# A recurrence and a long convolution on one core: states decimated by two, spilled to DRAM, and the two branches interleaved

## The chip, the cores and the metric

The kernel runs on one core of a Trainium2 chip. The metric is the device time of one execution in microseconds (us), as the median of several runs. The engines are called TensorE (PE in the profile; PEld is its weight load), VectorE (DVE), ScalarE (ACT), GpSimd (POOL) and SyncE (SP). In this kernel SyncE computes nothing: it issues nearly all DMAs, in program order.

## The reference, cut to what matters

The output mixes two branches over a sequence of 2048 steps and 1024 channels in bf16. Branch A (called S5 below) is a complex diagonal recurrence. Branch B multiplies a 4-tap shift convolution of k with v and runs the product through a 2048-long convolution, by a transform of length 4096. A gate per time step mixes them.

```python
g = sigmoid((x * gate_w).sum(-1, keepdims=True))
# branch A (S5)
Lam_bar = exp(dt * Lam);  B_bar = ((Lam_bar - 1) / Lam)[:, None] * Bmat
Bu = einsum("bld,pd->blp", x, B_bar)
for t in range(L):                       # 2048 steps, 1024 complex states
    h = Lam_bar * h + Bu[:, t, :]
a = 2 * einsum("blp,dp->bld", hseq, Cmat).real + x * Dskip
# branch B (convolution)
kv = shift_conv4(k, shift_k) * v
y  = irfft(rfft(pad(kv)) * rfft(pad(ssm_k)))[:, :S] + kv * ssm_D
b  = x * y
out = g * a + (1 - g) * b
```

## The kernel before

It computes branch B first and branch A after it, in two separate phases.

The convolution works on eight units of 128 channels. Each unit has a first transform stage (`stage1`), a spectrum stage (`spec`), a product on VectorE, an inverse (`inverse`) whose result is spread over partitions by DMA into `zb`, and a final stage. All PSUM tiles come from one pool of four, and their evictions are split between VectorE ("V") and ScalarE ("A").

```python
with tc.tile_pool(name="bpsum", bufs=4, space=PSUM) as bpsum, ...:
    def inverse(pp, zb, q, eng):
        ps = bpsum.tile([128, 4, 2, CH], F32, name="ps")
        ...                                              # [cut: 12 matmuls]
        qq = bW.tile([128, 4, 2, CH], BF16, name="qq")   # pool bW: 2 buffers
        evac(eng, qq, ps)
        for i in range(4):
            nc.sync.dma_start(out=zb[...], in_=qq[:, i]...)
    ...
    for u in range(NU):                                  # 8 units
        zb = bZ.tile([128, 16, 2, CH], BF16, name="zb")  # pool bZ: 2 buffers
        for q in range(4):
            spec(z, kv, q, 0, "A")
            stage1(a, zs[u + 1], w, 2 * (q % 2), "V")
            ...                                          # [cut]
            inverse(*pend, "A")
            final(zb_prev, u - 1, q - 2, "V" if q == 2 else "A")
```

Then comes the recurrence, in four time blocks of 512 steps. C is transposed whole and scaled; each block runs the input GEMM, rotates *every* step on VectorE, scans it, rotates it back, and runs the output GEMM from states that never leave SBUF:

```python
for pi in range(NP):
    ...                                                  # [cut] CrT, CiT: 16 transposes, 4 x 8 scalings on ScalarE
for tb in range(NTB):                                    # 4 time blocks
    for pi in range(NP):                                 # 8 state blocks
        ...                                              # [cut] 16 input matmuls, 2 evictions
        nc.vector.tensor_tensor(out=t1, in0=tbc, in1=bure, op=ALU.mult)        # rotate: 6 ops of 512
        ...
        nc.vector.tensor_tensor_scan(out=Wre, data0=rcol_bc, data1=pre_re, initial=init_re, ...)
        nc.vector.tensor_tensor_scan(out=Wim, data0=rcol_bc, data1=pre_im, initial=init_im, ...)
        ...                                              # rotate back: 6 ops of 512
    for tl in range(TT_B):
        ...                                              # [cut] output GEMM of a time tile, gate, store
```

## Time and profile before

| | before |
|---|---|
| time, median of 2 runs | 644.14 us (643.22 to 645.06) |
| TensorE busy | 410.0 us, 64% |
| VectorE busy | 465.4 us, 72% |
| ScalarE busy | 306.4 us, 48% |
| moved by DMA | 59.4 MB |

Lines of the page of the kernel before. The first lines give busy time and share of each engine; the next four show, in 40 equal slices of the span (16 us each), the busy tenths of TensorE and VectorE, the granted TensorE clock in tenths, and the busy share of the DMA engines; the last is a group of instructions (busy us, mean ns | idle before them, and what ended it).

```profile
span 643.4 us, 6726 instructions
...
PE 410.0 (64%) x2240; PEld 212.4 (33%) x2240; DVE 465.4 (72%) x1059; ACT 306.4 (48%) x415; POOL 4.1 (1%) x10
...
PE   0023877484747493953451087999699978998577
...
DVE  7649997393939462630372389999999899989952
...
PEclk9999997778887888876875578999889998999579
DMA  9899705564749364135994022041204200110001
...
L283 DVE CAST zkv<-ps 128x1024 bf16<-128x1024 f32 x28 | 34.2, 1220 | 50.0 <-PE ps L327 49.8
```

The window table of the same kernel, by stage: length of the window, then busy us of each engine with its instruction count, the granted clock, the DMA share and the rate.

```profile
core 0: us, PE busy (x) PEld busy (x) DVE busy (x) ACT busy (x) POOL busy (x), PEclk, DMA share, GB/s
0.00:41.00 41.00, 0.00 (x0) 0.00 (x0) 21.47 (x63) 22.20 (x26) 4.10 (x10) 1.00 0.94 146
41.00:298.00 257.00, 156.10 (x1080) 104.66 (x1080) 168.42 (x267) 134.56 (x139) 0.00 (x0) 0.85 0.58 123
298.00:372.00 74.00, 23.20 (x76) 8.28 (x77) 28.92 (x62) 50.05 (x61) 0.00 (x0) 0.64 0.60 120
372.00:622.00 250.00, 213.42 (x1005) 91.82 (x1005) 240.67 (x655) 92.75 (x180) 0.00 (x0) 0.91 0.16 49
```

What TensorE waited for in the convolution stage of the same kernel (total us, times, longest):

```profile
engine line waited for: us in total, times, longest us
PE ps L327 <- DMA va<-kv_scr: 55.7, 6, 13.1
...
PE ps L374 <- DMA zb<-qq: 20.5, 5, 5.8
```

The tables are read together. Between 41 and 298 us the convolution runs alone and no engine is busy for more than two thirds: it is a chain of waits (reload of `va`, arrival of `zb`), and the clock is granted at 0.85 only. Between 372 and 622 us VectorE is busy 240.7 of 250 us: it is the bound there. So each phase leaves idle what the other needs.

A measure used below is *column work*: the moving columns of all matmuls in a window times 0.216 us per 512 columns, the spacing of matmuls at the full clock in this trace. The kernel before has about 346 us of it in 643 us.

### The profile page before, as it was taken

What the parts mean: (1) busy time and instruction counts of PE and PEld (TensorE: products, weight loads), DVE (VectorE), ACT (ScalarE), POOL (GpSimd) and SP (SyncE); (2) the same over time, 40 slices, a digit from 0 to 9 for tenths busy, and PEclk for the clock granted to TensorE, in tenths of its full rate; (3) what the DMA queues carried; (4) which work ended last, traced back from release to release, by engine and by line L of the source; (5) the groups of instructions that cost most, each with busy time, mean ns of one, the idle gap of its engine ahead of it and who ended that gap; (6) DMA issues with size and microseconds to landing.
All of it is one profiled execution on the core that took longest, in us unless ns stands there. A gap on an engine that the chain in (4) does not pass through costs nothing.

```text
span 643.4 us, 6726 instructions
## 1 busy us (share of the span) xinstructions
PE 410.0 (64%) x2240; PEld 212.4 (33%) x2240; DVE 465.4 (72%) x1059; ACT 306.4 (48%) x415; POOL 4.1 (1%) x10
## 2 busy tenths in 40 slices
PE   0023877484747493953451087999699978998577
PEld 0011654252424362631110033344244433443133
DVE  7649997393939462630372389999999899989952
ACT  3832865454454664741369961264126611552042
POOL 2000000000000000000000000000000000000000
PEclk9999997778887888876875578999889998999579
DMA  9899705564749364135994022041204200110001
GB/s 173 154 163 254 164 26 131 120 143 100 162 84 175 70 131 89 43 98 103 169 201 116 17 83 59 7 131 66 63 4 130 83 0 1 52 64 0 2 16 49
DMA packets 166026, 59.44 MB, mean 92 GB/s; under 512 B 142312, under 2 KB 158696, under 8 KB 165992
## 3 DMA queue, kind: packets, MB, share of 16 engines
q1 hardware_dynamic: 157312, 54.54, 39.6%
q10 hardware_dynamic: 8680, 4.48, 2.8%
q8 instruction: 17, 0.28, 0.2%
q14 instruction: 17, 0.14, 0.1%
HBM read 17.06 MB, written 12.58 MB: 46 GB/s over the span
## 4 chain that ended last, share of the span: by engine, by line
DVE 41%; PE 21%; ACT 11%; DMA 9%; SPq 9%; issue 5%; ACTq 0%; DVEq 0%
DVE Wim L575 5%; DVE Wre L573 5%; DMA va<-kv_scr 4%; SPq L363 4%; PE ps L336 3%; ACT kv L285 3%; PE ps L327 3%; DVE acc L306 2%; PE psy L607 2%; PE psy L604 2%; PE ps L356 2%; SPq L491 2%; DVE pre_re L549 2%; DVE pre_im L555 2%; DVE hb_re L584 1%
## 5 line engine op out<-in xcount | busy, mean ns | idle before, releaser
L285 ACT CAST kv<-ps 128x1024 bf16<-128x1024 f32 x64 | 64.3, 1015 | 65.8 <-PE ps L338 58.3
L283 DVE CAST zkv<-ps 128x1024 bf16<-128x1024 f32 x28 | 34.2, 1220 | 50.0 <-PE ps L327 49.8
L327 PE MATMUL ps<-tab_188,va 128*128 128x256 bf16 x128 | 25.4, 341 | 57.5 <-DMA va<-kv_scr 55.7
L336 PE MATMUL ps<-zkv,fC 128*128 128x512 bf16 x128 | 54.7, 428 | 6.2 <-ACT kv L285 4.9
L604 PEld LDWEIGHTS <-hb_re 128*128 128x128 bf16 x256 | 25.7, 102 | 76.2 <-DVE hb_re L584 46.1
L285 ACT CAST qq<-ps 128x1024 bf16<-128x1024 f32 x32 | 32.5, 1019 | 32.1 <-DMA zb<-qq 29.6
L327 PE MATMUL ps<-tab_188,ka 128*128 128x256 bf16 x128 | 20.9, 295 | 42.0 <-DVE ka L321 41.4
L285 ACT CAST zkv<-ps 128x1024 bf16<-128x1024 f32 x36 | 36.1, 1022 | 22.1 <-PE ps L327 22.0
L607 PEld LDWEIGHTS <-hb_im 128*128 128x128 bf16 x256 | 26.1, 103 | 47.6 <-issue 18.4
L542 ACT ACTIVATE bure<-bu_re 128x512 bf16<-128x512 f32 x32 | 19.1, 597 | 47.3 <-PE bu_re L535 18.5
L613 ACT ACTIVATE m_t<-dsk,gcols 128x512 bf16<-128x512 bf16 x32 | 23.1, 723 | 35.6 <-DVE u_t L617 32.7
L611 ACT ACTIVATE ga<-psy,gcols 128x512 bf16<-128x512 f32 x32 | 21.3, 676 | 38.6 <-PE psy L607 37.5
L337 PE MATMUL ps<-zkv,fS 128*128 128x256 bf16 x128 | 38.4, 300 | 0.0
L338 PE MATMUL ps<-zkv,fN 128*128 128x256 bf16 x128 | 38.3, 299 | 0.0
L356 PE MATMUL ps<-pp,gC 128*128 128x256 bf16 x128 | 32.5, 288 | 8.6 <-ACT kv L285 5.0
L327 PEld LDWEIGHTS <-va 128*128 128x128 bf16 x128 | 14.9, 120 | 64.2 <-DMA va<-kv_scr 57.5
L374 PE MATMUL ps<-zb,tabFc 128*128 128x512 bf16 x32 | 15.1, 473 | 28.7 <-DMA zb<-qq 28.7
L573 DVE TENSOR_TENSOR_SCAN Wre<-rv,init_re,pre_re 128x512 bf16<-128x512 f32 x24 | 30.6, 1276 | 0.0
L575 DVE TENSOR_TENSOR_SCAN Wim<-rv,init_im,pre_im 128x512 bf16<-128x512 f32 x24 | 30.5, 1271 | 0.0
L543 ACT ACTIVATE buim<-bu_im 128x512 bf16<-128x512 f32 x32 | 19.1, 596 | 22.5 <-PE bu_im L538 22.5
L306 DVE TENSOR_TENSOR acc<-acc,tmpj 128x2047 bf16<-128x2047 bf16 (+2 forms) x24 | 29.3, 1222 | 0.5
L357 PE MATMUL ps<-pp,gN 128*128 128x128 bf16 x128 | 29.2, 228 | 0.0
(793 smaller groups left out, 1153.3 us busy)
## 6 DMA issues: line engine op xcount, KB each, us to landing
zb<-qq SPq DMA_DIRECT2D x128, 64.0 KB
ka<-in_B_ssm_k_dram SPq DMA_DIRECT2D x8, 512.0 KB
kv_scr<-acc SPq DMA_DIRECT2D x8, 512.0 KB
va<-kv_scr SPq DMA_DIRECT2D x8, 512.0 KB
pB_scr<-cv SPq DMA_DIRECT2D x16, 256.0 KB
out_dram<-ot SPq DMA_DIRECT2D x16, 256.0 KB
pbb<-pB_scr ACTq DMA_DIRECT2D x8, 256.0 KB
x_tt<-in_A_x_dram SPq DMA_DIRECT2D x8, 256.0 KB
```

The source lines that it names most:

```text
L283: nc.vector.tensor_copy(o, i_)
L285: nc.scalar.copy(o, i_)
L306: nc.vector.tensor_tensor(out=acc[:, j:S], in0=acc[:, j:S], in1=tmpj[:, 0:S - j], op=ALU.add)
L327: nc.tensor.matmul(ps[:, i, :], lhsT=a[:, 4 * q + i, :], rhs=t1v, start=True, stop=True)
L336: nc.tensor.matmul(ps[:, i], lhsT=fC[:, k2, :], rhs=z[:, k2], start=True, stop=False)
L337: nc.tensor.matmul(ps[:, i, :, 0, :], lhsT=fS[:, k2, :], rhs=z[:, k2, :, 1, :], start=False, stop=False)
L338: nc.tensor.matmul(ps[:, i, :, 1, :], lhsT=fN[:, k2, :], rhs=z[:, k2, :, 0, :], start=False, stop=True)
L356: nc.tensor.matmul(ps[:, i], lhsT=gC[:, k2, :], rhs=pp[:, i], start=True, stop=False)
L573: nc.vector.tensor_tensor_scan(out=Wre, data0=rcol_bc, data1=pre_re, initial=init_re, op0=ALU.mult, op1=ALU.add)
L575: nc.vector.tensor_tensor_scan(out=Wim, data0=rcol_bc, data1=pre_im, initial=init_im, op0=ALU.mult, op1=ALU.add)
L604: nc.tensor.matmul(psy, lhsT=hb_re[:, pi, tl * 128:(tl + 1) * 128], rhs=CTr[pi][:, d0:d0 + DHW], start=(cnt == 0), stop=(cnt == n_mm - 1))
L607: nc.tensor.matmul(psy, lhsT=hb_im[:, pi, tl * 128:(tl + 1) * 128], rhs=CTi[pi][:, d0:d0 + DHW], start=(cnt == 0), stop=(cnt == n_mm - 1))
```

## The change

Its intent is to let the two branches fill each other's gaps. The recurrence is decimated by two: only even steps are rotated and scanned on VectorE, and TensorE makes the odd ones by small diagonal matrices. The input GEMM runs state block by state block over all time, so each finished block of states has to be spilled to DRAM and reloaded for the output GEMM. The convolution units are written between the recurrence's pieces, at a fixed ratio of estimated work. The diff is a rewrite; this is its core, with cuts marked and comments added here:

```diff
-            tc.tile_pool(name="bpsum", bufs=4, space=bass.MemoryType.PSUM) as bpsum:      # convolution
-         tc.tile_pool(name="apsum", bufs=2, space=bass.MemoryType.PSUM) as apsum:         # recurrence, later
+    psum = ctx.enter_context(tc.tile_pool(name="psum", bufs=2, ...))    # names psS and psB: 2 buffers a branch
...
-        for tb in range(NTB):
-            for pi in range(NP):
-                ...                               # [cut] rotate, scan and rotate back all 512 steps
+        for pi in range(NP):                       # one state block, all 2048 steps
+            for c in range(NC):
+                gemm_u(BT, dg, Hc, 1, c)           # odd inputs
+                yield 3.5
+                if tail is not None:
+                    odd(*tail, c)                  # odd states of the block before, then spill
+                    yield 1.3
...
+                gemm_u(BT, dg, Hc, 0, c)           # even inputs + coupling of the odd ones
...
+                rot(Hc, pi, c, tabs, wl)           # rotate and scan the even steps only
...
+    def odd(dg, Hc, pi, c):
...
+            nc.sync.dma_start(out=h_scr[pi, c], in_=Hc[c].rearrange("p a b s -> p (a b s)"))   # spill, 0.5 MB
...
+        for pi in order:                           # after the last block
+            load_CT(0, pi)                         # two 512 x 128 transposes
+            for c in range(NC):
+                nc.sync.dma_start(out=Hs[pi][:, c].rearrange(...), in_=h_scr[pi, c])           # reload, 0.5 MB
+        for i in range(4):
+            load_CT(1, order[i])
...                                                # 2 x 16 output tiles; xn, pb loads and ot store on SyncE
-                evac(eng, qq, ps)                  # convolution evictions on VectorE or ScalarE
+        nc.scalar.copy(qq, ps)                     # all on ScalarE; qq has 2 buffers, zb has 1
...
+    TOT_S, TOT_C = 190.0, 123.0
+    for w in sg:                                   # pieces of the recurrence
+        done_s += w
+        while cg is not None and done_c < TOT_C * done_s / TOT_S:
+            step = next(cg, None)                  # pieces of the convolution
```

## The prediction

> **What bounds the kernel now.** It runs in four stages (windows by stage). 0-41 us: set-up, no matmul; the first waits 41.4 us. 41-298 us: convolution alone; TensorE 156, VectorE 168, ScalarE 135 us busy of 257, so no engine is full. The waits are a latency chain: ScalarE on the spectrum matmuls 58 us, TensorE on the reload of kv from DRAM 56 us. The granted clock is 0.85, and matmuls after a gap run at half rate: 128x512 start every 0.43 us at 227 us, every 0.216 us in a full stretch. 298-372 us: transition, TensorE 23 us busy; ScalarE scales C (32 x 1.13 us). 372-622 us: recurrence, VectorE-bound (241 of 250 us; scans 1.2 us each, 512-wide multiplies 0.34 apart).
>
> **What the change does.** The two branches are interleaved, so recurrence work can fill the convolution's gaps and keep the array warm. The Trainium skill, "TensorE: Matmul & The Clock Gate", part 1, says the clock is halved after an idle window of about 3.4 us; this trace agrees (0.43 against 0.216 us after an 8.5 us wait).
>
> Engine sums after, costed with trace durations (estimates):
> - TensorE: 0.216 us per 512 columns at full rate. Input and output GEMMs 524,288 columns as before; convolution 294,912 as before; new: diagonal scaling of B 32,768, odd-to-even coupling 32,768, odd-state reconstruction 49,152, gates 16,384. 950,000 columns, about 400 us (before: about 346).
> - VectorE: only even steps are rotated and scanned: 16 x about 6.7 us = 107 (before about 230); shift convolution 63, products 61, output 40, final stage 20, tables and parameters 20: about 310 (before 465). The 28 evictions of 1.22 us leave it.
> - ScalarE: 1.02 us per 1024-wide eviction: about 255 (before 306); the C scaling goes.
> - DMA: about 76 MB (before 59), with 8.4 MB of states written and read back; about 70% of the rate implied by the present share.
>
> So the bound moves from VectorE and latency to TensorE.
>
> **Critical path, predicted.**
> - Start: x transposed (16 x 1.3 us issue), the parameter chain (done at 22 us now), table generation on ScalarE and VectorE, the kv round trip: about 43 us, with 8 us of TensorE work done.
> - Eight interleaved blocks: TensorE 33, VectorE 31, ScalarE 28 us each. Three nearly equal engines in order will not overlap perfectly: about 37 us, 290 in all.
> - Turn to the output GEMM: 8.4 MB of states and 2 MB of C transposes must land before the first accumulation ends. Large rows: 1 MB at 341 GB/s in "DMA: Bandwidth & Descriptors", Bandwidth; this trace shows 254 GB/s at best. 30-40 us of transfer, about 18 us of it a bubble.
> - Output: 110 us GEMM plus 16 us left of the convolution, plus a 6 us bubble where C's second half reuses buffers.
> - Tail 3 us.
>
> Sum: about 480 us, a gain of 25%. Range 445 to 525. Faster by over 2%: 0.96; within 2%: 0.02; slower: 0.02.
>
> **What would show it.** TensorE's mean clock above 0.93 and its busy share above 80%; VectorE near 310 us and ScalarE near 255 us; no matmul-free stage between the two branches except one of 10-30 us where states are reloaded, its waits named on the state reload; output stage at about 3.5 us a tile; DMA share 60-75%.
>
> **What would make it wrong.** Slower: DMA queues congested by spill, transposes and 256-byte rows, so that convolution loads wait; two PSUM buffers per branch serialising matmul and eviction; GpSimd operations slowed beside VectorE; head-of-line waits in the single issuing queue. Faster: blocks at TensorE's own 33 us and a hidden reload would give about 440.

## The result

| | before | after | predicted |
|---|---|---|---|
| time, median | 644.14 us | 604.58 us (603.71 to 605.44, 2 runs) | 480 us (445 to 525) |
| ratio to before | 1 | 0.939 (95%: 0.934 to 0.944) | 0.745 |
| TensorE busy | 410.0 us, 64% | 463.6 us, 77% | above 80% |
| mean granted clock, profiled run | 0.862 | 0.904 | above 0.93 |
| VectorE busy | 465.4 us | 351.7 us | 310 us |
| ScalarE busy | 306.4 us | 250.3 us | 255 us |
| DMA moved | 59.4 MB | 80.5 MB | 76 MB |

Ratios here and below are the mean time of one kernel's fast runs over the mean of the other's fast runs of the same rounds, so they are not quite the ratios of the medians quoted.

The change is faster, but by 6% and not by 25%. Lines of the page of the changed kernel, as above:

```profile
span 603.7 us, 7373 instructions
...
PE 463.6 (77%) x2720; PEld 244.4 (40%) x2720; DVE 351.7 (58%) x636; ACT 250.3 (41%) x278; POOL 132.9 (22%) x98
...
PE   0554896988799878978979938646826698879996
...
DVE  2967699395935788597698792232201372723432
...
PEclk9977897998899998998999989679757889898999
DMA  9996932622229216566386194168983454644331
...
L565 ACT CAST z<-psB 128x1024 bf16<-128x1024 f32 x64 | 62.5, 1029 | 12.6 <-PE psB L563 12.6
```

The slices are 15.1 us each here. From slice 5 to slice 23 it is what was intended: TensorE mostly at 7 to 9 tenths and VectorE busy beside it. From slice 24 on (about 350 us) TensorE swings between 2 and 8 tenths for nine slices, VectorE has little to do, and only the last eight slices are full again. Of the 64 evictions of the first stage, 28 were on VectorE before, at 1.22 us each; all 64 are now on ScalarE, at 1.03 us.

The window table of the changed kernel:

```profile
core 0: us, PE busy (x) PEld busy (x) DVE busy (x) ACT busy (x) POOL busy (x), PEclk, DMA share, GB/s
0.00:66.00 66.00, 29.26 (x148) 15.50 (x149) 43.21 (x112) 29.68 (x40) 20.55 (x21) 0.87 1.00 168
66.00:349.60 283.60, 249.48 (x1621) 138.19 (x1619) 215.80 (x394) 168.79 (x186) 61.06 (x38) 0.95 0.48 110
349.60:410.00 60.40, 34.38 (x238) 21.19 (x237) 24.87 (x40) 28.23 (x30) 6.12 (x3) 0.80 0.59 149
410.00:450.00 40.00, 24.39 (x150) 13.67 (x150) 7.86 (x16) 14.81 (x15) 0.00 (x0) 0.78 1.01 285
450.00:519.00 69.00, 50.52 (x236) 23.14 (x236) 27.42 (x34) 8.82 (x9) 22.99 (x17) 0.85 0.47 121
519.00:603.70 84.70, 75.61 (x332) 32.76 (x331) 32.51 (x43) 0.00 (x0) 22.16 (x19) 0.96 0.39 112
```

The blocks (66 to 349.6 us) run at a granted clock of 0.95 with TensorE busy 88% of the time. From 349.6 to 519 us no engine is busy more than about three quarters, and the clock is granted at 0.78 to 0.85. Between 410 and 450 us the DMA share is 1.01: the engines are full. In numbers of column work:

| window, us | length | column work | without column work |
|---|---|---|---|
| 0-66 start and first block | 66.0 | 22.1 | 43.9 |
| 66-349.6 blocks | 283.6 | 223.3 | 60.3 |
| 349.6-450 turn | 100.4 | 41.5 | 58.9 |
| 450-519 output beside convolution | 69.0 | 42.3 | 26.7 |
| 519-603.7 output alone | 84.7 | 71.7 | 13.0 |

SyncE's issues at the turn, in order of time, from the timeline of the changed kernel (start us, length us, line, operation, out<-in, count):

```profile
396.63 2.53 SPq L600 DMA_DIRECT2D zb<-qq  x4
399.20 0.93 SPq L316 DMA_DIRECT2D h_scr<-Hc  x2
400.17 2.14 SPq L406 DMA_TRANSPOSE CT<-in_A_C_re_dram  x1
404.30 2.08 SPq L620 DMA_DIRECT2D pB_scr<-xs  x2
407.02 2.55 SPq L600 DMA_DIRECT2D zb<-qq  x4
409.62 2.17 SPq L406 DMA_TRANSPOSE CT<-in_A_C_im_dram  x1
411.90 0.99 SPq L414 DMA_DIRECT2D Hr<-h_scr  x2
412.94 1.14 SPq L406 DMA_TRANSPOSE CT<-in_A_C_re_dram  x1
...
449.85 0.58 SPq L428 DMA_DIRECT2D xn<-in_A_x_dram  x1
...
451.01 1.27 SPq L600 DMA_DIRECT2D zb<-qq  x2
```

The last odd matmul starts at 363.3 us and its eviction ends at 364.9 us, but the last two spills are issued only at 399.2 us: SyncE's order has the convolution's `zb` stores before them, and those wait for the convolution (between 349.6 and 450 us SyncE waited 20.3 us for copies into `qq` and 9.0 us for the final stage's results). C's transposes and the reloads then go on without a gap from 409.6 us until the first of the output's own loads, `xn`, is issued at 449.9 us; only after that come the next `zb` stores. A transpose of 512 rows takes 1.20 to 1.26 us to issue (medians of the line), a reload of 0.5 MB 0.48 us. In this stretch stand 23 of C's 32 transposes (one went ahead, eight come later) and all 16 reloads: 28 and 8 us of issue by the medians, 36 of the 40 us. In bytes it is 11.4 MB (285 GB/s times 40 us).

What ScalarE waited for from 349 to 520 us in the changed kernel:

```profile
engine line waited for: us in total, times, longest us
ACT qq L597 <- PE psB L595: 36.1, 4, 30.6
ACT qq L597 <- DMA zb<-qq: 25.3, 1, 25.3
```

One copy into `qq` waited 25.3 us for a DMA: its two buffers were still to be stored to `zb`, and those stores stood in SyncE's order behind the loads. The trace shows no other instruction on ScalarE during that wait (433.6 to 458.9 us): all evictions of the convolution behind that copy waited with it.

### The profile page after: what moved, and what is told of

It reads as the page before. It is cut to its first block, busy times and chain, and to the rows that moved or that the text cites. A ratio compares the mean times of both kernels' runs of the same rounds, so it can differ in the third digit from the quotient of the medians.

```text
span 603.7 us, 7373 instructions
## 1 busy us (share of the span) xinstructions
PE 463.6 (77%) x2720; PEld 244.4 (40%) x2720; DVE 351.7 (58%) x636; ACT 250.3 (41%) x278; POOL 132.9 (22%) x98
## 5 line engine op out<-in xcount | busy, mean ns | idle before, releaser
L434 PE MATMUL psS<-CT,Hr 128*128 128x512 bf16 x512 | 125.2, 403 | 30.8 <-DVE ot L441 20.8
L261 PE MATMUL psS<-xT,BT 128*128 128x512 bf16 x512 | 129.3, 393 | 7.1 <-ACT Hc L315 3.3
L434 PEld LDWEIGHTS <-Hr 128*128 128x128 bf16 x512 | 51.9, 102 | 101.3 <-issue 43.1
L576 ACT CAST kv<-psB 128x1024 bf16<-128x1024 f32 x64 | 65.1, 1032 | 29.3 <-PE psB L575 24.3
L261 PEld LDWEIGHTS <-BT 128*128 128x128 bf16 x512 | 50.2, 101 | 63.8 <-issue 17.9
L565 ACT CAST z<-psB 128x1024 bf16<-128x1024 f32 x64 | 62.5, 1029 | 12.6 <-PE psB L563 12.6
L429 POOL TENSOR_TENSOR xn<-xn,dsk 128x512 bf16<-128x512 bf16 x32 | 37.6, 1177 | 128.7 <-DMA xn<-in_A_x_dram 115.4
L573 PE MATMUL psB<-z,fC 128*128 128x512 bf16 x128 | 50.3, 393 | 7.3 <-ACT z L565 4.6
L272 ACT CAST Hc<-psS 128x1024 bf16<-128x1024 f32 x32 | 32.3, 1011 | 39.9 <-PE psS L261 14.7
L313 PE MATMUL psS<-Hc,dg 128*128 128x512 bf16 x64 | 24.6, 437 | 20.3 <-DVE Hc L305 19.7
L553 DVE TENSOR_TENSOR acc<-acc,tmpj 128x1024 bf16<-128x1024 bf16 (+3 forms) x48 | 35.5, 739 | 0.9
L574 PE MATMUL psB<-z,fS 128*128 128x256 bf16 x128 | 35.7, 279 | 0.0
L575 PE MATMUL psB<-z,fN 128*128 128x256 bf16 x128 | 35.7, 279 | 0.0
L315 ACT CAST Hc<-psS 128x1024 bf16<-128x1024 f32 x16 | 16.5, 1032 | 43.4 <-PE psS L313 43.4
```

Source lines behind the costliest of these rows:

```text
L261: nc.tensor.matmul(ps[:, ri, :], lhsT=BT[:, d, ri, :], rhs=xT[d][:, par, c0:c0 + CW], start=(d == 0), stop=(par == 1 and d == ND - 1))
L429: nc.gpsimd.tensor_tensor(out=xn, in0=xn, in1=dsk[:, ds_], op=ALU.mult)
L434: nc.tensor.matmul(ps[:, ti, :], lhsT=Hs[pi][:, a // 4, par, ri, (a % 4) * 128:(a % 4 + 1) * 128], rhs=CT[dh, pi][:, ri, :], start=(i == 0 ...
L553: TT(out=acc[:, lo:hi], in0=acc[:, lo:hi], in1=tmpj[:, 0:hi - lo], op=ALU.add)
L565: nc.scalar.copy(z[:, :, w, :, 64 * q:64 * q + 64].rearrange("p k r (g c) -> p k r g c", c=8), ps.rearrange("p g (k r c) -> p k r g c", r= ...
L573: nc.tensor.matmul(ps[:, i], lhsT=fC[:, k2, :], rhs=zz, start=True, stop=False)
```

## The experiments

The theories. **Latency and interlock (L, later C):** each branch is a chain of latencies; put into fixed in-order streams, each holds the other up, above all where leftover convolution meets the output GEMM. **The queue or its transfers (O, later T):** what is lost at the turn is the issue time of one queue, or the bytes behind it. **VectorE (V):** the shift convolution's small taps delay the scan in each block. The expectations name these theories by letter or in words. There are eighteen runs of seventeen kernels: the last one, e18, turned out to be e16 again. The results of all but those marked as wrong are correct. Several runs fall outside both ranges of their expectation. For orientation, read from the traces (start times in us; the "last convolution matmul" is the last one of `L617` or the line that it became, and its partner starts 0.2 to 0.5 us later):

| run | last even input matmul | first output matmul | last convolution matmul | last output matmul | last output minus last even |
|---|---|---|---|---|---|
| the change | 349.3 | 425.6 | 515.8 | 599.5 | 250.2 |
| e1 wide C | 351.6 | 430.0 | 521.5 | 599.4 | 247.8 |
| e2 ScalarE queue | 350.2 | 409.6 | 544.4 | 610.4 | 260.2 |
| e3 half reload | 348.6 | 426.0 | 510.6 | 594.2 | 245.6 |
| e4 convolution earlier | 394.8 | 470.2 | 469.4 | 627.9 | 233.1 |
| e5 wide and half | 353.0 | 430.8 | 512.4 | 588.2 | 235.2 |
| e6 convolution later | 341.6 | 419.4 | 562.9 | 635.8 | 294.2 |
| e7 later, wide, GpSimd | 340.6 | 435.5 | 566.1 | 630.8 | 290.2 |
| e9 zb on ScalarE | 392.1 | 415.2 | 542.4 | 604.0 | 211.9 |
| e10 GpSimd queue | 349.3 | 414.5 | 551.4 | 629.2 | 279.9 |
| e11 no taps | 333.2 | 409.6 | 501.5 | 584.3 | 251.1 |
| e13 C hoisted | 352.2 | 434.6 | 508.2 | 588.6 | 236.4 |
| e14 and 3 blocks kept | 348.5 | 372.0 | 505.6 | 584.1 | 235.6 |
| e15 four copies | 346.8 | 412.6 | 501.8 | 585.8 | 239.0 |
| e16 e14 and 3 copies | 346.8 | 365.5 | 484.0 | 564.9 | 218.1 |
| e17 e13 and 3 copies | 346.3 | 419.2 | 494.2 | 572.5 | 226.2 |
| e18 the kernel of e16 again | 346.8 | 365.7 | 482.9 | 561.3 | 214.5 |

One count is needed for several runs. A spectrum group is one group of spectrum matmuls; there are 128 in all, 16 a unit. Before the last odd matmul the traces show 88 groups in the change and in every run except four: 104 in e4, 72 in e6 and e7, 106 in e9 (e8 and e12, each with one branch only, aside). The count is the same 88 without the taps (e11) and with more copies (e15), so it is not set by how fast a run goes. It is the order of the built program: the kernel file of the change writes 106 groups there, and its built program has 88, because the framework reorders instructions when it builds.

### e1: C in 16 wide transposes instead of 32 half-wide ones

```diff
-            t = cp.tile([128, 2, 512], BF16, name="CT", bufs=12)
+            t = cp.tile([128, 2, D], BF16, name="CT", bufs=8)
-                nc.sync.dma_start_transpose(out=t[:, ri, :], in_=src[dh * 512:(dh + 1) * 512, pi * 128:(pi + 1) * 128])
+                nc.sync.dma_start_transpose(out=t[:, ri, :], in_=src[:, pi * 128:(pi + 1) * 128])
```

> C is transposed in 16 full-width issues (128x1024) instead of 32 half-width ones (128x512); bytes are the same and all of C lies in place before the output stage. Theory Q (the single issuing queue sets the turn from the blocks to the output GEMM: 32 half-width transposes took about 1.2 us each there, 40 us with the state reloads, and everything behind them waits): 16 issues of about 1.3 us instead of 32 of 1.2, so 15 to 19 us less at the turn, and the 9 us bubble in the middle of the output stage (537 to 546 us) goes: about 578 us (570 to 585). Theory B (the turn is bound by DMA throughput, since its DMA share is about 1.0 at 285 GB/s): only the 9 us bubble goes, about 595 us.

Measured: 600.8 us (598.12 to 605.22), ratio 0.933 (0.929 to 0.938). Sixteen transposes instead of 24 before the output's first load gave 4 us at most, and the interval overlaps the change's own. The stretch from the first of C's transposes of imaginary parts to the first `xn` load is 41 us (413.2 to 454.4), as before: the transposes of imaginary parts now took 2.8 us each (median) to issue while the DMA engines were full, those of real parts 1.16 us. The number of issues alone is not the limit. One thing did go as expected: the gap in the middle of the output (two output tiles start 9.2 us apart at 535.4 us in the change) is gone, every tile there following after about 3.5 us. But the first output matmul comes 4.4 us later, and 600.8 us lies above theory B's 595 too.

### e2: reloads and output transfers on ScalarE's queue

```diff
-                nc.sync.dma_start(out=Hs[pi][:, c]..., in_=h_scr[pi, c])
+                nc.scalar.dma_start(out=Hs[pi][:, c]..., in_=h_scr[pi, c])
```

and the same for the loads of xn and pb and the output store.

> State reloads, and the loads and stores of the output stage, are issued from ScalarE's queue; the C transposes and the convolution's transfers stay on the first queue. Same bytes. Theory Q: loads no longer stand behind transposes and behind stores that wait for convolution results: 15 to 35 us less, 570 to 590 us, and the gaps between output tiles from 450 to 519 us shrink. Theory B: no change beyond 5 us, 600 to 609 us.

Measured: 614.74 us (613.01 to 619.67), ratio 0.955 (0.949 to 0.961): slower than the change. The output GEMM began 16 us earlier, but the convolution ended 29 us later: a copy into `z` stood 40.8 us on ScalarE, where the issues had to wait for a transfer of C. A second queue on an engine that computes moves the head-of-line wait there.

### e3: only half of the states reloaded (wrong)

```diff
-            for c in range(NC):
+            for c in range(1):
-    lhsT=Hs[pi][:, a // 4, par, ri, ...]
+    lhsT=Hs[pi][:, 0, par, ri, ...]
```

> Wrong result on purpose: only half of the states is read back (4.2 MB less, 8 issues of 0.5 us less), and the output GEMM uses that half twice. Theory B: 4.2 MB at the 285 GB/s of the turn is 15 us less, about 590 us. Theory Q: 8 issues, about 4 us less, about 600 us.

Measured: 602.31 us (598.72 to 607.1), ratio 0.936 (0.930 to 0.941). Taking away 4.2 MB of about 11 changed nothing that the interval shows. The stretch is 35.5 us (410.2 to 445.7): eight reload issues are gone, and the rest is mostly the issue time of the transposes. Bytes alone are not the limit either. (Where an expectation counts 32 transposes in this stretch, it should be 24: the last eight are issued in the middle of the output.)

### e4: the convolution written earlier

```diff
-    TOT_S, TOT_C = 190.0, 123.0
+    TOT_S, TOT_C = 150.0, 123.0
```

> The constant that paces the convolution against the recurrence goes from 190 to 150, so that in the instruction order all convolution matmuls stand before the first output matmul (before, 262 of 1024 output instructions stood among them). Theory T (the left-over of the convolution, 2.5 of 8 units at the end of the blocks, is the cost: latency-bound alone from 365 to 410 us and interlocked in order with the output GEMM from 450 to 519 us): the blocks grow by about 15 us, the rest shrinks by 30 to 50 us, so 570 to 590 us. If the queue alone matters (theory Q), the blocks grow and the turn stays, 600 to 620 us.

Measured: 632.18 us (628.17 to 633.85), ratio 0.981 (0.976 to 0.985). That is above both ranges. With no convolution left beside the output GEMM, what follows the blocks shrinks by 17 us (250.2 to 233.1), but the blocks end 45 us later, and the turn is not hidden: of the 61 us from 408.5 to 470 us, 36 had no column work, of the next 40 us 33. Convolution between the blocks is not free, and the loads at the turn are a hole that leftover convolution partly fills. From the last odd matmul to the first output matmul it is 62 us, as in the change.

### e5: e1 and e3 together (wrong)

The edit is the two above together.

> Wrong result on purpose: the full-width C transposes of the first experiment and the halved state read-back of the third in one kernel. Each alone left the 40 us load stretch (410 to 450 us) as long as it was: with half the bytes it is held by 32 issues of 1.2 us, with half the issues by bytes (a full-width transpose then took 2.7 us on a full DMA). Theory D (two limits of equal size lie on the same stretch, issue and bytes): both relieved, the stretch shrinks to about 25 us and the bubble in the middle of the output stage goes, 575 to 588 us. Theory S (the load stretch is hidden behind what is left of the convolution, which runs until 519 us anyway): 595 to 602 us, no more than either alone.

Measured: 591.65 us (591.19 to 594.12), ratio 0.919 (0.916 to 0.923). This lies between the ranges of D and S. Either relief alone gave 2 to 4 us, both together 13 us. From SyncE's timeline of this run:

```profile
413.52 2.48 SPq L406 DMA_TRANSPOSE CT<-in_A_C_im_dram  x1
416.11 0.52 SPq L413 DMA_DIRECT2D Hr<-h_scr  x1
416.68 1.18 SPq L406 DMA_TRANSPOSE CT<-in_A_C_re_dram  x1
...
444.85 0.43 SPq L422 DMA_DIRECT2D xn<-in_A_x_dram  x1
```

The stretch is now 31.3 us (413.5 to 444.9) instead of 40.2. Fewer issues alone left it at 41.2 us, fewer bytes alone at 35.5. So it has two limits that lie close together, the issue of the transposes and the bytes, and relieving one leaves the other. The 9 us of the stretch are not the whole gain of 13: the gap in the middle of the output is gone as in e1, some 6 us.

### e6: the convolution written later

```diff
-        while cg is not None and done_c < TOT_C * done_s / TOT_S:
+        goal = 86.0 * done_s / 164.5 if done_s < 165.0 else 86.0 + (done_s - 164.5) * (127.0 - 86.0) / 46.0
+        while cg is not None and done_c < goal:
```

> The convolution is written later into the program: 5.5 of 8 units by the end of the blocks (the change: 6.6; executed there: 5.5), the rest spread over the first 13 output tiles. The last spill and the first C load then stand behind 80 stores of inverse transforms in the issuing queue, not 96. Theory O (the queue is in order, and the turn starts 35 us late, at 400 us, because it stands behind stores of convolution units that the execution has not reached at 365 us): the loads start at about 370 to 380 us, the output GEMM 20 to 30 us earlier, 570 to 590 us. Theory T (left-over convolution in the output stage costs by interlocking): more is left over, so it is slower, 605 to 630 us.

Measured: 640.81 us (638.19 to 647.69), ratio 0.997 (0.989 to 1.004). That is above both ranges. The blocks end 8 us sooner, and what follows them is 44 us longer. The edit left more undone than the expectation says: 72 groups, four and a half units, stand before the last odd matmul, not five and a half. And the loads did not start sooner after it: the first output matmul still comes 62 us behind the last odd one. Leftover convolution beside the output GEMM is dearer than in the blocks. Together with e4, the pacing of the change stands near an optimum in both directions.

### e7: later, with wide C and reloads on GpSimd's queue

The edits of e1 and e6, and the reloads issued by GpSimd.

> The late pace, the full-width C transposes, and the state reloads issued from GpSimd's queue, which is empty there. Theory O with theory D: 560 to 580 us. Theory T: no gain, 600 us or more.

Measured: 637.83 us (636.8 to 638.12), ratio 0.990 (0.987 to 0.993). What e6 lost is not brought back. But the run does not show why, since the loads were not relieved: beside GpSimd's reloads the first transpose of C took 13.9 us to issue, and the first output matmul came 16 us later than in e6 (435.5 against 419.4).

### e8: the recurrence alone (no convolution; wrong)

```diff
-    cg = conv_gen()
+    cg = None
# [cut] the output stage loads x in place of the convolution's result
```

> Wrong result on purpose: the convolution units are left out (the shift convolution stays), so the recurrence branch runs alone. If the blocks of the change are bound by TensorE's own work: 8 blocks of about 20 us, last block at about 215 us instead of 363; the turn, with nothing else in the queue, about 45 us of loads; output 115 us; in all 370 to 390 us. If the recurrence chain (evictions, rotation, scan) binds a block by latency instead, blocks of 30 us or more and 450 us in all.

Measured: 438.61 us (435.65 to 441.58), one round. Its windows (start, blocks, turn, output):

```profile
27.00:258.00 231.00, 184.48 (x835) 83.02 (x836) 186.70 (x338) 90.28 (x98) 46.95 (x33) 0.89 0.42 107
258.00:318.00 60.00, 20.05 (x50) 4.97 (x48) 11.79 (x23) 3.04 (x3) 2.95 (x3) 0.55 0.76 223
318.00:438.30 120.30, 109.22 (x480) 47.57 (x478) 47.22 (x62) 0.00 (x0) 34.65 (x30) 0.95 0.36 107
```

Alone, the blocks take 29 us each for about 20 us of column work (161.6 in 231 us), with VectorE busy 186.7 of 231 us. At the turn TensorE is busy 20 of 60 us at a clock of 0.55, although no store of a convolution stands in SyncE's way. From the last odd matmul (269.5 us) to the end there are 168.8 us with 110.8 us of column work: 58 us of idle time belong to this branch's own turn and output. Here the output GEMM begins 9 us after the last odd matmul (278.3 us) and then waits 22.1 us, in eight pieces, for reloads (`Hr`): the sign that the prediction named.

### e9: the zb transfers on ScalarE's queue

```diff
-            nc.sync.dma_start(out=zb[k2:128:16]...,
+            nc.scalar.dma_start(out=zb[k2:128:16]...,
```

> The 128 transfers that turn the inverse transform's output around (zb from qq) are issued from ScalarE's queue, right behind the eviction that makes qq, so that the main queue no longer waits for ScalarE (94 us of its waits in the change). Nothing else moves. Theory O (in-order waits in the one issuing queue hold back the loads at the turn and slow the convolution, and the two together cause the lost time from 350 to 519 us): 20 to 45 us less, 560 to 585 us, C loads from about 370 us. Theory L (both branches are latency chains over PSUM buffers and in-order engines; the queue is a symptom): within 10 us of 605, and ScalarE's 77 us of extra issue may even cost.

Measured: 612.76 us (609.91 to 614.53), ratio 0.949 (0.946 to 0.953). What follows the blocks falls by 38 us, to 211.9, and the blocks end 43 us later. Not all of this is the queue's doing. The built order changed with the edit: 106 groups stand before the last odd matmul instead of 88, so convolution moved from the end into the blocks. The fair comparison is e4, with 104 groups and blocks that end 45 us later: against it, what follows the blocks is 21 us shorter. The turn itself shows the queue: without the `zb` stores before them, spills and loads issue sooner, and the first output matmul comes 10 us after the last odd one instead of 62 (in e4 also 62). On the other side, ScalarE's `kv` evictions now waited 51.1 us, in 14 pieces, for `zb` transfers. So the shared queue does cost time at the turn, and ScalarE is a poor place to put the stores.

### e10: reloads and output transfers on GpSimd's queue

The edit is that of e2 with `nc.gpsimd`.

> State reloads and the output stage's loads and stores are issued from GpSimd's queue; C transposes and all convolution transfers stay on the main queue. In the second experiment the same moved to ScalarE's queue cost 10 us, and there ScalarE's evictions waited 41 us behind a load. Theory O: the output tiles no longer stand behind convolution stores from 450 to 519 us, 10 to 25 us less, 580 to 595 us. Theory L: 600 us or more.

Measured: 632.84 us (630.29 to 636.32), ratio 0.981 (0.977 to 0.985). The output GEMM begins 11 us earlier and ends 30 us later. A part of it stands in the trace: behind GpSimd's reloads two of C's transposes take 9.6 and 5.1 us to issue on SyncE, and after its first two matmuls the output GEMM stands still for 24 us, the last 10.0 of them put down to a transfer of C. How the rest divides is not shown.

### e11: the three shifted taps left out

```diff
-        for j in range(1, KS):
+        for j in range(1, 1):
```

The result still lies within the tolerance, since the taps are small, but it is not the reference's computation.

> Wrong result on purpose: the three shifted taps of the short convolution are left out, about 61 us of VectorE's 352, 7 us in each of the first blocks. If VectorE's in-order stream sets the pace of the blocks (theory V: 29 us per block alone against 20 us of TensorE work, because rotation and scan wait behind the taps): blocks 5 to 6 us shorter, 565 to 580 us. If TensorE or the PSUM buffers do: less than 10 us gained.

Measured: 586.37 us (585.12 to 590.24), ratio 0.908 (0.905 to 0.911). It lies between the two expectations. About 61 us of VectorE instructions are gone, and the last even matmul comes 16 us sooner, 2 us per block; what follows the blocks is unchanged (251.1). VectorE's taps cost the blocks something, but nothing at the turn, and the 18 us gained are less than a third of what was removed.

### e12: the convolution alone (no recurrence; wrong)

```diff
-        for pi in range(NP):
+        for pi in range(0):
-        for pi in order:
+        for pi in ():
-                    for i, pi in enumerate(order):
+                    for i, pi in ():
# [cut] C is not loaded, the shift convolutions and the gates are made first, the output is written without the recurrence
```

> Wrong result on purpose: the recurrence blocks, spill, C loads and output GEMM are left out; short convolution, gates, all 8 convolution units and a copy of the result to the output remain. Before, the convolution alone took about 30 us a unit with 15 us of TensorE work. Theory L: again about 30 us a unit, so the units end at about 310 us and the whole takes about 340 us; together with the 438 us of the recurrence alone that makes 780 us less the start (45) and the common parts, so that the change's 604 us overlaps only part of the two chains. If the unit alone runs at TensorE's rate: units end at about 190 us.

Measured: 445.26 us (443.05 to 447.46), one round. Its convolution window, and TensorE's longest wait:

```profile
65.00:376.00 311.00, 176.30 (x1301) 115.65 (x1300) 146.50 (x246) 152.68 (x156) 35.81 (x21) 0.79 0.52 112
```

```profile
PE psB L618 <- DMA zb<-qq: 47.0, 6, 10.9
```

This is far above both expected times (340 us in all, or units done at 190 us). Eight units take 311 us, 39 us each, for about 15.5 us of column work; in the kernel before a unit took about 30 us, with four PSUM buffers, evictions on two engines and two `zb` buffers. The final stage alone waits 47.0 us for `zb`. So neither branch alone is near TensorE's pace: 439 and 445 us alone, 604 together. Interleaving saved 279 us of their sum (in which the common start is counted twice) and could not hide the rest.

### e13: C's first half hoisted into the last two blocks

The first 16 transposes are written into blocks 6 and 7, into space that the shift convolution has left; the second half is loaded one at a time during the first output tiles. All states are still reloaded.

```diff
+                if pi >= 6:
+                    load_CT(ep, 0, 4 * (pi - 6) + 2 * c)
+                    load_CT(ep, 0, 4 * (pi - 6) + 2 * c + 1)
-            load_CT(0, pi)
-        for i in range(4):
-            load_CT(1, order[i])
+                    if dh == 0 and ti == 1:
+                        load_CT(cp, 1, order[tp])
```

> The first half of C is transposed and scaled during the last two blocks, in space freed by the short convolution; the second half is transposed and scaled during the first eight output tile pairs, one at a time. Between the last block and the first output tile only the 8.4 MB of reloaded states are left. The results stay correct. Theory T (the stretch between blocks and output is set by transfers: bytes at about 285 GB/s and about 1.2 us of issue for each of 32 transposes, both near 40 us): the issue limit is gone, the byte limit falls from about 12 MB to 8.4 MB, so the load stretch takes about 29 us instead of 40, and the time is 585 to 596 us, with the first output GEMM near 412 instead of 426. Theory C (the convolution units left over at the end of the blocks are a latency chain of their own, which goes on for some 150 us whatever the loads do): the first output GEMM is earlier, but the last convolution matmul stays within 8 us of 499 and the time is 597 us or more.

Measured: 593.17 us (590.3 to 594.64), ratio 0.918 (0.915 to 0.922). The time lies in T's range, but T's first output matmul (412 us) does not come: it comes at 434.6 us. The last spectrum matmul is at 491.1 us, 8 us sooner. Neither theory holds alone. The trace says why the first output matmul is late. The 16 hoisted transposes were not issued inside the blocks: eight are issued from 361.3 us and eight from 395.5 to 412.0 us, after the last even matmul (352.2) and among the convolution's stores. The reloads then take 14.7 us instead of a stretch of 40, but they begin at 419.7 us. So the hoist emptied the load stretch, and its late start stayed. The expectation says that C is also scaled; it is not (C is only transposed in the changed kernel), which changes no number in it.

### e14: e13, and the states of blocks 5 to 7 kept in SBUF

```diff
-            nc.sync.dma_start(out=h_scr[pi, c], in_=Hc[c]...)
+            if pi < 5:
+                nc.sync.dma_start(out=h_scr[pi, c], in_=Hc[c]...)
-        order = list(range(NP))
+        order = [5, 6, 7, 0, 1, 2, 3, 4]
# [cut] the five reloads are written before the last odd states; pools changed to keep Hc and dg
```

> As the run before, and the states of blocks 5 to 7 stay in SBUF instead of going through DRAM, so that 5.2 MB instead of 8.4 MB come back, and the output GEMM takes the kept blocks first. Correct results. Theory T: the load stretch falls to about 18 us and a part of it hides under the last odd GEMMs; time 560 to 580 us. Theory C: 590 us or more; the last convolution matmul no earlier than 488.

Measured: 591.14 us (590.16 to 592.87), ratio 0.917 (0.914 to 0.919). The output GEMM begins at 372 us, 54 us sooner than in the change, and the time is that of e13 (0.917 against 0.918). That is in C's range. But the early start is only that of the kept blocks: after it the output GEMM stands still for 35.5 us, and its first matmul on a reloaded state comes at 413.7 us. ScalarE's waits from 347 to 509 us in this run:

```profile
engine line waited for: us in total, times, longest us
ACT qq L605 <- DMA xn<-in_A_x_dram: 31.2, 1, 31.2
```

A copy into `qq` now waits 31.2 us. The profile puts its end down to an `xn` load of the output; the `zb` stores before it were issued in ones to threes between the output's loads and stores, from 444.8 to 466.2 us. How the 31.2 us divide is not shown. The convolution ends at 505.6 us, 10 us sooner than in the change.

### e15: four buffers for the inverse's eviction instead of two

```diff
-        qq = bW.tile([128, 4, 2, CH], BF16, name="qq")
+        qq = bW.tile([128, 4, 2, CH], BF16, name="qq", bufs=4)
```

> The inverse transform's eviction buffer gets 4 copies instead of 2, nothing else. In the change ScalarE waited about 94 us in all, and the SyncE queue as long, around these copies, and a PSUM buffer of the convolution stays taken while the copy waits. Theory C with the pinned PSUM buffer as its largest link: 585 to 598 us, and more than 5.5 units done by the end of the blocks. Theory C with the chain of 16 stores and the single buffer of the final transform as its link, or theory T: 600 to 607 us, no change that the interval separates from zero.

Measured: 592.65 us (591.79 to 595.7), ratio 0.919 (0.916 to 0.922). One word gives 12 us, in the range of the pinned buffer. ScalarE's waits from 349 to 450 us:

```profile
engine line waited for: us in total, times, longest us
ACT Hc L315 <- PE psS L313: 12.0, 2, 6.9
ACT qq L597 <- PE psB L595: 11.3, 4, 8.4
```

No copy waits for a DMA any more, and the last spectrum matmul comes at 485.3 instead of 498.7 us. The other half of that expectation failed: 88 groups are done by the end of the blocks, as in the change (17 of the 128 records of `L573` are missing, but those of `L574` and `L575` are complete). So the gain is at the turn. The Trainium skill, "Perfetto Trace Analysis", Optimization Strategy, says that a gap that repeats can mean that there aren't enough buffers for the next tile; here too few buffers showed as one long wait (25.3 us) and not as a repeated gap, and two more gave 12 us.

### e16: e14 with three copies (four don't fit)

```diff
# e14's edits, and
-        qq = bW.tile([128, 4, 2, CH], BF16, name="qq")
+        qq = bW.tile([128, 4, 2, CH], BF16, name="qq", bufs=3)
```

> The two together (3 copies, as 4 don't fit), as the version that should beat both kernels. If the gains add: 550 to 575 us. If both shorten the same wait: within 5 us of the better one of the two.

Measured: 569.38 us (567.36 to 573.29), ratio 0.883 (0.879 to 0.887): 35 us less than the change, more than the 13 and 12 us of the two alone. Its windows:

```profile
347.00:385.00 38.00, 25.48 (x182) 15.03 (x184) 20.50 (x38) 20.69 (x22) 2.14 (x2) 0.82 0.51 106
385.00:487.00 102.00, 76.78 (x429) 39.17 (x436) 40.69 (x56) 28.42 (x30) 23.80 (x17) 0.89 0.69 168
487.00:569.20 82.20, 73.88 (x325) 32.72 (x330) 33.53 (x45) 0.00 (x0) 24.10 (x20) 0.98 0.40 111
```

From 347 us on, 71 us have no column work, against 99 us in the change after its last block. (49 of this trace's 2720 matmul records are missing, 10.6 us of column work, so 71 is too high; the complete trace of the same kernel, e18's, has 64.) The convolution ends at 484 instead of 515.8 us.

### e17: e13 with three copies

```diff
# e13's edits, and
-        qq = bW.tile([128, 4, 2, CH], BF16, name="qq")
+        qq = bW.tile([128, 4, 2, CH], BF16, name="qq", bufs=3)
```

> C's first half hoisted into the last two blocks (all states still reloaded) and 3 copies of the inverse transform's eviction buffer. Each alone gave about 13 us (0.918 and 0.919 of the time before, against 0.939 for the change). If the two gains are independent: 578 to 583 us. If they shorten the same wait: 588 to 593 us. If, as with the kept states, each was held back by the other: below 575 us. It also tells how much of the 569 us of the run before is due to the kept states themselves (5.2 MB instead of 8.4 MB to reload).

Measured: 579.79 us (578.48 to 581.18), ratio 0.899 (0.896 to 0.901). The two gains add: from the change's 0.939, 0.021 for the hoisted C and 0.020 for the copies give 0.898. The kept states are worth nothing without the copies (e13 to e14: 0.918 to 0.917) and 10 us with them (e17 to e16: 0.899 to 0.883; 14 us in the rounds of e17 itself, where the kernel of e16 ran as e18 with 0.878). So their gain depended on the copies. That they were off the critical path until the convolution was released is the reading that fits; it was not traced.

### e18: meant as e16 with the convolution written earlier; in fact e16 again

The edit described below (190 to 150 in e4, here 190 to 170) was not made: the kernel that ran is e16's, byte for byte.

> The best version with the convolution written about one ninth earlier against the recurrence. In the change itself writing it earlier (190 to 150) cost 28 us because the blocks stretched and then the bare turn came on top. With the turn shortened and the copies no longer held, the leftover convolution is what remains between 385 and 487 us, some 39 us without column work; if it is the limit now, an earlier convolution gains: 555 to 566 us. If the pacing is still at its optimum: 569 to 580 us.

Measured: 566.54 us (565.53 to 567.42), ratio 0.878 (0.875 to 0.880). Nothing follows from it about the pacing, which stays untested on this version. What it gives is a second measurement of e16 on another chip: 0.878 against 0.883. The same kernel can differ by 3 us between two sets of rounds, so differences of that size between runs (e1, e3, e13 to e14) are not to be read. The kernel of e16 is the fastest of all in both.

## Why the prediction was wrong

The direction was right, and so were the engines' sums: column work was predicted at about 400 us and is 401; ScalarE at 255 and is 250 us; DMA at 76 and is 80.5 MB. VectorE was 42 us above its sum (351.7 against 310); taking 61 us of its instructions away (e11) gained 18. Wrong was the time in which TensorE would have nothing to do: the terms of the prediction imply 88 us, and there are 203.

The prediction's terms add up to 486 us, which it rounded to 480. Against the profiled run of 603.7 us:

| term of the prediction | predicted | measured | difference |
|---|---|---|---|
| start and eight blocks, to the last even matmul | 43 + 290 = 333 | 349.3 | +16 |
| last odd states after it | none | 14.2 | +14 |
| column work after that | 110 + 16 = 126 | 152.1 | +26 |
| idle after that | 18 + 6 + 3 = 27 | 88.1 | +61 |

The sum of the differences is 117 us, the whole of 603.7 minus 486.

- **Start and blocks: nearly the right length, by luck.** "About 37 us" a block was close, but with less convolution in it. In idle time this step failed as well: to the last even matmul the terms imply 61 us without column work (35 in the start, 26 in the blocks), and there are 104. The prediction had seven of eight units done by the end of the blocks ("16 us left of the convolution"); the trace has 88 of 128 spectrum groups, five and a half units, by 363 us. That share is the order of the built program, as said above; the prediction took the order as written. Whether more convolution would have fitted into blocks of this length was not shown: e12 speaks against it, since with two PSUM buffers, all evictions on ScalarE and one `zb` buffer a unit takes 39 us by itself, not the 15.5 us of its column work. (The 47.0 us of waits for `zb` are measured there; what the PSUM buffers and the evictions each add is argued, not tested.) e11 shows that VectorE's taps are worth 2 us a block.
- **The step that failed most is the turn and the output: "30-40 us of transfer, about 18 us of it a bubble", then "110 us GEMM plus 16 us left of the convolution, plus a 6 us bubble".** The transfer itself was sized well: 40 us for the load stretch. Three things were not seen.
  - The load starts late. The last states are there at 365 us, the loads fill the DMA engines from 410 us. The last spill stands in SyncE's order behind stores that wait for the convolution. e9 shows it from the other side: with these stores elsewhere, the first output matmul follows the last odd one after 10 us instead of 62, and what follows the blocks is 21 us shorter than in e4, which has nearly as many spectrum groups done by then (104 against 106).
  - The bubble is not 18 us even without any convolution. e8 has 58 us of idle time between its last odd matmul and its end, where the prediction had 27: 31 of the 61 us.
  - The remaining 30 us of the 61 (88 less 58) come with the leftover convolution. While the loads are issued, its stores wait; so its copies wait 25.3 us on ScalarE; so its spectrum matmuls wait; so its result reaches the output tiles late, one tile per about 7 us between 450 and 519 us. e15 shows a part of this chain alone (12 us from two more buffers). e13 to e14 and e17 to e16 show that the kept states gain nothing without more copies and 10 to 14 us with them.
- **The expected signs.** The prediction looked for waits "named on the state reload". They were there for 5.6 us (TensorE on `Hr` between 349 and 519 us); the long waits were on VectorE's output step (19.5 us) and, on ScalarE, on `qq`. The clock was to be above 0.93 and is 0.904, because it falls to 0.78 to 0.85 in the 170 us after the blocks. The Trainium skill, "TensorE: Matmul & The Clock Gate", part 1, ties the clock to recent busyness; this trace agrees (0.95 in the blocks, 0.78 where TensorE is busy 24 of 40 us).
- **Where the prediction named it.** Its list of what would make it wrong has "two PSUM buffers per branch serialising matmul and eviction" and "head-of-line waits in the single issuing queue". The second occurred; the first was not tested by itself; neither had been given a number in the sum.

Rivals that fell: the queue's issue time alone (e1), the bytes alone (e3), VectorE at the turn (e11). A second queue for the loads, as tried in e2 and e10, made it slower, which does not clear the one queue, as e9 shows. What stood: the late start of the loads (e9, e13), two limits close together at the load stretch (e5), and the convolution's chain held by it (e15 to e17). What stays open: e16's kernel still has about 64 us without column work after its last block (e18's trace); how they divide between the recurrence's own turn and the convolution's single `zb` buffer was not separated, since a second `zb` buffer doesn't fit in SBUF (its kernel doesn't build with one). How the 28 us of GpSimd's queue (e10) divide is open too. The parts "31" and "30" are differences between two kernels' idle times, so they are a division by one experiment (e8) and not two separately tested causes.

## What to carry to other kernels

Before adding up engine sums for an interleaved kernel, time each stream alone: two latency chains of 439 and 445 us do not become their TensorE sum of 401 us. At a turn between stages, ask what stands ahead of the first new load in the issuing queue, and which buffers stay pinned while the queue is busy with it. Where two limits are close together, relieving one shows little; relieve both before ruling either out. And check in the trace that an edit did what it says: here the built order differed from the written one (88 groups, not 106), the hoisted transposes stayed at the turn (e13), and one edit was never made (e18).

## What the Trainium skill lacked or had wrong

- "DMA: Bandwidth & Descriptors", Issuing engines are not separate DMA queues, says that issuing from several engines saves only issuing time, "which is usually small relative to the DMA itself". Here it was as large: 1.20 to 1.26 us to issue a 512-row transpose of 128 KB, 36 of the 40 us of the stretch for all issues, so that fewer bytes alone gave nothing that the interval shows (e3). It agrees in that the second queue brought nothing (614.7 us on ScalarE's, 632.8 us on GpSimd's, against 604.6), but that section does not say that issues on a computing engine hold up that engine's own stream (ScalarE's evictions waited 40.8 us in e2 and 51.1 us in e9).
- The same page, DMA Transpose (X-bar), has no issuing time by shape for this chip. The runs show 1.20 to 1.26 us for 512 rows (medians); with 1024 rows, 1.16 us for half of them and 2.8 us for the other half while the DMA engines were full (e1); and single ones of 9.6 and 13.9 us beside reloads from GpSimd's queue (e10, e7).
- The same page, Bandwidth, gives 341 GB/s for 1 MB, for loads issued from GpSimd; no run here measures that case. It has no rate for loads mixed with transposes: the stretch of 0.5 MB reloads and transposes, issued from SyncE, reached 285 GB/s at a DMA share of 1.01.
- "Perfetto Trace Analysis", Optimization Strategy, says that interleaving regimes with different bounds may improve performance. That section does not mention that in-order streams couple them: the two branches alone take 439 and 445 us, together 604, of which 203 us still have no column work.
